# Batch 0 of a linear-attention + MLP kernel: half of Q moved to the GpSimd queue as bf16, and one attention step of batch 1 placed later

## The chip, the cores and the metric

The kernel runs on one core of a Trainium2 chip. The metric is the device time of one execution in microseconds (us); lower is better. The core has a matrix engine (TensorE, "PE", with its weight loads shown apart as "PEld"), a vector engine (VectorE, "DVE"), a scalar engine (ScalarE, "ACT"), a general engine (GpSimd, "POOL") and a sync engine ("SP"). SP, ACT and POOL issue DMA transfers. Transfers that change fp32 to bf16 on the way are all issued by POOL here.

## What is computed

```python
def attention(q, k, v, g_norm):            # batch 8, heads 8, seq 576, head_dim 64
    kv  = einsum('bhsd,bhse->bhde', k, v)
    out = einsum('bhsd,bhde->bhse', q, kv)
    rms = sqrt(mean(out * out, axis=-1, keepdims=True) + 1e-6)
    return out / rms * g_norm

x = attention(...).transpose(0, 2, 1, 3).reshape(4608, 512)
h = x @ w_in                               # 512 -> 2048
g = where(h > 0, h, exp(min(h, 0)) - 1)    # ELU
y = g @ w_out                              # 2048 -> 512, fp32
```

All inputs and the output are fp32 in DRAM. The matrix products run on bf16 copies.

## The kernel before, in words

The 4608 tokens are cut into nine token tiles of 512: the first 512 tokens of each of the eight batches, and one tile that collects the last 64 tokens of every batch. A token tile goes through attention, then `mm1` (the product with w_in: 64 matmuls of 128x512, in eight pieces of eight), ELU, and `mm2` (the product with w_out, 64 matmuls). The order of instructions on each engine is the order in which the Python code emits them; no scheduler changes it. While PE works on the mm1 and mm2 of one tile, the attention steps of the next are put between the pieces.

**The head** is everything before the first mm1 product of batch 0. Q of batch 0 (512 tokens of 8 heads) is brought as fp32 by two transfers of the sync queue, four heads each (`q_raw0`, tile `st_q`, L555). `cast_first` makes bf16 of it on DVE and ACT, one pair of heads at a time, into `q_two`. `turn_first` transposes a pair on PE with four 128x128 transposes (L622), and DVE copies the result from PSUM into `qT0`: pairs 0 and 2 by one copy (L631), pairs 1 and 3 later by `turn_last` (L695). K and V of batch 0 come through POOL, cast to bf16 on the way, as four K chunks and four V chunks of two heads each (`fetch_packed_kv`, L118). Behind them in the same queue stand w_in in seven slices (`load_w_in`, L136), the first part of w_out, Q of batch 1, more of w_out, K and V of batch 1, and so on. POOL has at most eight such transfers under way: the ninth waits until the first has landed, and so forth.

For each of four chunks c of heads PE forms K^T V (`kv_first`, L174, 18 small matmuls), DVE casts it to bf16 (L648), PE multiplies it with `qT0` (`se_first`, L654), ACT squares the scores (`square_first`, L663), PE takes the mean over a head (`mean_first`, L666), ACT takes ln and exp (`log_first` L669, `exp_first` L672), and DVE scales (`scale_first`, L675) and so writes `xT` for the chunk. Chunks 0 and 1 use pairs 0 and 2 of `qT0`, chunks 2 and 3 use pairs 1 and 3. The first 24 mm1 matmuls of batch 0 are emitted by `first` (L684), which starts as soon as chunk 0 of `xT` is there; the other 40 are L467. `idle` (L603) emits matmuls on zeros that nothing reads.

**Batch 1's attention** is interleaved with mm2 of batch 0 (L784 to L820). mm2 is cut by the contraction: `mm2_quarter(0, j, i)` for the first eight slices of w_out, then `mm2(0, j, 8, 10)`, `(10, 12)`, `(12, 14)`, `(14, 16)`, each for the four token groups j. Between these stand `q` (PE transposes of Q, L185), `kvu0`/`kvu1` (K^T V of half the heads each, L174), `seu0`/`seu1` (scores, L373), `sq`, `sum`, `inv`, `mul` (normalising) and `xu0`/`xu1` (PE transposes of the result, L413). POOL's queue brings batch 1's Q, K, V and the slices of w_out in the order in which this stretch uses them.

**The tail** is the last token tile's mm2 (L924): 80 matmuls in five output pieces, each copied out of PSUM by ACT (L932) and stored by two transfers, one from SP and one from ACT (L934). The last two pieces have 256 columns each.

Of the kernel before, what the change touches and what calls it, by code (L numbers as in the profile page):

```python
# [8 lines left out]
FP32 = mybir.dt.float32  # L9
BF16 = mybir.dt.bfloat16  # L10
# [6 lines left out]
def kernel(  # L17
# [13 lines left out]
    nc = tc.nc  # L31
    P = 128

    B, H, S, D = q.shape
    DM = H * D
    DF = moe_w_in.shape[1]
    NPAIR = H // 2
    J = 4
    G = J * P
# [7 lines left out]
    packed = ctx.enter_context(tc.tile_pool(name="packed", bufs=2))  # L47
# [9 lines left out]
    ident = const.tile([P, P], BF16, name="ident")  # L57
# [10 lines left out]
    def stage_tile(tag):  # L68
        return stage.tile([P, 2304], FP32, name=f"st_{tag}", tag=tag)
# [38 lines left out]
    def packed_kv(b):  # L108
        for name, pool in (("k", packed), ("v", qkvp)):
            t = pool.tile([P, 4, RK, D], BF16, name=f"{name}_pk", tag=name)  # L110
            raw[name, b] = t
            bf[name, b] = t.rearrange("p h j d -> p j h d")

    def fetch_packed_kv(name, b, hs=slice(0, 4)):
        in_ = (k if name == "k" else v)[b].rearrange("h r d -> (h r d)").rearrange(
            "(h p x) -> p h x", h=4, p=P
        )
        nc.gpsimd.dma_start(  # L118
            out=raw[name, b].rearrange("p h j d -> p h (j d)")[:, hs], in_=in_[:, hs]
        )  # L120
# [25 lines left out]
    def copy_on(eng, out_, in_):  # L146
        if eng is nc.scalar:
            nc.scalar.copy(out_, in_)
        else:
            eng.tensor_copy(out=out_, in_=in_)  # L150
# [17 lines left out]
    def kv_single(T, kv_ps, u, ls=(0, 1)):  # L168

        for j in range(RK):  # L170
            for l in ls:
                for s in range(2):
                    rows = slice(s * 64, s * 64 + 64)
                    nc.tensor.matmul(  # L174
                        kv_ps[l * 64 : l * 64 + 64, s, u * 64 : u * 64 + 64],
                        lhsT=bf["k", T][rows, j, 2 * u + l, :],
                        rhs=bf["v", T][rows, j, 2 * u + l, :],
                        start=(j == 0),
                        stop=(j == RK - 1),
                    )  # L180
# [328 lines left out]
    def mm2(T, j, f0, f1, hold=False):  # L509

        if f0 == 0 and (T, j) not in o_ps:
            o_ps[T, j] = ps_m2.tile([P, DM], FP32, name="o_ps", tag="mm2")
        for f in range(f0, f1):
            nc.tensor.matmul(  # L514
                o_ps[T, j],
                lhsT=gT[T][:, f, j * P : j * P + P],
                rhs=w_out_sb[:, f, :],
                start=(f == 0),
                stop=(f == FC - 1),
            )  # L520
        if f1 == FC and not hold:
            mm2_out(T, j)

    def mm2_out(T, j):
        if j % 2 == 0:
            o_sb[T] = outp.tile([P, 2, DM], FP32, name="o_sb", tag="o")
        nc.scalar.copy(o_sb[T][:, j % 2, :], o_ps.pop((T, j)))  # L527
        if j % 2 == 1:
            store(T, j // 2)
# [20 lines left out]

    V, A, Q = nc.vector, nc.scalar, nc.gpsimd

    q_raw0 = stage_tile("q")[:, 0:2048].rearrange("p (u x) -> p u x", u=2)
    for u in range(2):
        nc.sync.dma_start(  # L555
            out=q_raw0[:, u].rearrange("p (h x) -> p h x", h=4),
            in_=q[0, 4 * u : 4 * u + 4, 0:G, :].rearrange("h (p j) d -> p h (j d)", j=J),
        )
    packed_kv(0)
    for c in range(4):  # L560
        fetch_packed_kv("k", 0, slice(c, c + 1))
        if c == 2:
            make_identity(nc, ident)
        fetch_packed_kv("v", 0, slice(c, c + 1))
    edges = (0, 256, 512, 768, 1024, 1280, 1664, 2048)
    for lo, hi in zip(edges, edges[1:]):
        load_w_in(slice(lo, hi))
# [14 lines left out]
    for s in range(2):  # L582
# [5 lines left out]
        out=g_row,  # L588
        in_=bass.AP(tensor=g_norm.tensor, offset=g_norm.offset, ap=[[1, 1], [0, 2], [1, 64]]),
# [7 lines left out]
    def bank(n):  # L597
        return ps_head.tile([P, G], FP32, name=f"bank{n}", tag=f"bank{n}")

    def idle(ps, n, dtype=BF16):  # L600
        z = zeros.bitcast(dtype)
        for _ in range(n):
            nc.tensor.matmul(ps, lhsT=z[:, 0:P], rhs=z[:, 0:512], start=True, stop=True)  # L603
# [5 lines left out]
    idle_ps = bank(1)  # L609
    idle(idle_ps, 2, FP32)  # L610
    idle(idle_ps, 1)
    q_st = q_raw0.rearrange("p u (l s j d) -> p u s j l d", l=2, s=2, j=J)
    q_two = attp.tile([P, NPAIR, J, 2, D], BF16, name="q_two", tag="q_two", bufs=1)
    qT0 = attp.tile([P, NPAIR, G], BF16, name="qT", tag="qT")

    def cast_first(pair, eng):
        copy_on(eng, q_two[:, pair], q_st[:, pair % 2, pair // 2])

    def turn_first(ps, pairs):
        for r, pair in enumerate(pairs):  # L620
            for j in range(J):
                nc.tensor.transpose(ps[:, r, j * P : j * P + P], q_two[:, pair, j], ident)  # L622

    def turned(n):
        return bank(n).bitcast(BF16).rearrange("p (r t) -> p r t", r=2)

    cast_first(0, V)
    cast_first(2, A)
    qt_ps = turned(3)
    turn_first(qt_ps, (0, 2))  # L630
    nc.vector.tensor_copy(  # L631
        out=qT0.rearrange("p (s u) t -> p u s t", u=2)[:, 0], in_=qt_ps
    )
    idle(idle_ps, 1, FP32)
    cast_first(1, V)
    cast_first(3, A)

    kv0 = attp.tile([P, 2, 2, D], BF16, name="kv0", tag="kv0", bufs=1)
    x0 = attp.tile([P, KC, G], BF16, name="xT", tag="xT")
# [4 lines left out]
    def kv_first(c):  # L644
        u, l = c // 2, c % 2
        kv_single(0, kv_ps, u, (l,))
        ls = slice(l * 64, l * 64 + 64)
        nc.vector.tensor_copy(out=kv0[ls, u], in_=kv_ps[ls, :, u * 64 : u * 64 + 64])  # L648
# [13 lines left out]
    def square_first(c):  # L662
        nc.scalar.activation(sq0[c], se0[c], AF.Square)  # L663

    def mean_first(c):
        nc.tensor.matmul(mean0[c], lhsT=means, rhs=sq0[c], start=True, stop=True)  # L666

    def log_first(c):
        nc.scalar.activation(r0[c], mean0[c], AF.Ln, bias=eps_col)  # L669
# [4 lines left out]
    def scale_first(c):  # L674
        nc.vector.scalar_tensor_tensor(  # L675
            out=x0[:, c, :], in0=se0[c], scalar=g_col, in1=r0[c], op0=ALU.mult, op1=ALU.mult
        )
# [11 lines left out]
                    stop=(c == KC - 1),  # L689
                )  # L690

    def turn_last(n, pair):
        qt_ps = turned(n)
        turn_first(qt_ps, (pair,))
        nc.vector.tensor_copy(out=qT0[:, pair, :], in_=qt_ps[:, 0, :])  # L695

    g_ps = bank(2)
    nc.tensor.matmul(
        g_ps[:, 0:1],
# [3 lines left out]
        stop=True,  # L703
    )
    nc.vector.tensor_copy(out=g_col, in_=g_ps[:, 0:1])
    kv_first(0)
    turn_last(7, 1)
    se0[0] = bank(6)
    se_first(0)
    square_first(0)  # L710
    turn_last(0, 3)
    kv_first(1)
    mean0[0] = bank(2)
    mean_first(0)
    log_first(0)
# [5 lines left out]
    mean0[1] = bank(0)  # L721
    mean_first(1)
    log_first(1)
    idle_ps = bank(3)
    se0[2] = bank(1)
    se_first(2)
    square_first(2)
    exp_first(1)
    scale_first(0)
    idle(idle_ps, 1)  # L730
    kv_first(3)
    mean0[2] = bank(2)
    mean_first(2)
# [7 lines left out]
    pair = ps_head.tile([P, 2, G], FP32, name="h_ps", tag="kv")  # L741
# [25 lines left out]
    at, ahead = attention(1), attention(2)  # L767
    for i in range(3, 8):
        mm1(0, i, relu=i in (3, 5, 7), home={5: "m2", 6: "at"}.get(i, "m1"))()
    nc.gpsimd.tensor_copy(  # L770
        out=kv_sb[:, 0].rearrange("p (s u) e -> p u s e", s=2), in_=kv0
# [25 lines left out]
    at["mulu0"]()  # L797
    for j in range(J):
        mm2(0, j, 8, 10)
        if j == 2:  # L800
            at["kvu1"]()
    at["seu1"]()
    at["sq1"]()
    at["sum1"]()
    for j in range(J):
        mm2(0, j, 10, 12)
        if j == 1:
            at["inv1"]()
            at["xu0"](scores[:, 0, :])
# [4 lines left out]
        mm2(0, j, 12, 14)  # L814
    for j in range(J):
        mm2(0, j, 14, FC, hold=j > 1)
        if j == 0:
            at["xu1"](scores[:, 1, :])
    mm2_out(0, 2)
    mm2_out(0, 3)  # L820
# [57 lines left out]
    at, ahead = ahead, attention(3)  # L878
# [22 lines left out]
    for T in range(2, NT):  # L901
        at = ahead if T + 1 < NT else None
# [17 lines left out]
    for j, cols in pieces:  # L920
        n = cols.stop - cols.start
        ps = ps_m2.tile([P, DM], FP32, name="o_ps", tag="mm2")[:, 0:n]
        for f in range(FC):
            nc.tensor.matmul(  # L924
                ps,
                lhsT=gT[B][:, f, j * P : j * P + P],
                rhs=w_out_sb[:, f, cols],
                start=(f == 0),
                stop=(f == FC - 1),
            )  # L930
        sb = outp.tile([P, DM], FP32, name="o_last", tag="o_last", bufs=5)[:, 0:n]
        nc.scalar.copy(sb, ps)  # L932
        for l, eng in enumerate((nc.sync, nc.scalar)):
            eng.dma_start(out=rows[l, G:S, j, cols], in_=sb[l * 64 : l * 64 + 64, :])  # L934

# [29 lines left out]
```

## Time and profile before

| what | value |
|---|---|
| median of three runs | 284.0 us (283.41 to 284.29) |
| the profiled execution, its own time | 283.72 us |
| its span in the profile | 282.0 us |
| PE busy | 276.0 us, 98% of the span |
| DVE, ACT, POOL busy | 57%, 55%, 20% |
| chain of work that ended last | 94% PE, 2% DMA, 1% ACT |
| POOL's DMA queue (q0) | 17.30 MB written |
| sync and scalar queues (q1, q10) | 17.83 MB and 0.52 MB |

The span runs from the first to the last instruction of the program that the profiler shows; the execution's own time is 1.72 us longer. Bytes are counted where they are written, so a transfer that casts fp32 to bf16 reads twice what is shown. A row "idle before <-X" says how long an engine stood still before an instruction and what ended that.

### The profile page before, as it was taken

The page shows a single profiled execution, that of the slowest core. Times are in us where ns is not written, and L with a number is a line of the kernel's source. Part 1 is how long each engine was busy: PE and PEld are TensorE (multiplying, and loading weights), DVE is VectorE, ACT ScalarE, POOL GpSimd, SP SyncE. Part 2 cuts the span into 40 slices and gives each one's busy share as a digit, 9 for nine tenths or more (in the row PEclk, how much of TensorE's full clock was granted, in tenths as well). Part 3 has the DMA queues.
Part 4 walks back from the last instruction along what each step waited for, and adds up shares of the span by engine and source line. Part 5 has one row for each costly group of instructions (what it writes and reads, how often), then busy time and mean ns, then how long its engine had stood idle before and what let it go on. Part 6 is the DMA issues. An engine that isn't in the chain of part 4 may idle for free.

```text
span 282.0 us, 5163 instructions
## 1 busy us (share of the span) xinstructions
PE 276.0 (98%) x2134; PEld 129.8 (46%) x2134; DVE 159.8 (57%) x232; ACT 153.8 (55%) x221; POOL 56.2 (20%) x98
## 2 busy tenths in 40 slices
PE   7899999999999999999999999999999999999994
PEld 3444544445444444444444444444444444444444
DVE  2559453888388546843693469445854586444400
ACT  2679546666487438533863377337923692333311
POOL 7854422143421341004110421012000000000000
PEclk9999999999999999999999999999999999999999
DMA  7999999697796696359935795455236123010122
GB/s 196 199 200 202 208 201 191 179 170 128 178 177 114 157 157 156 74 149 121 198 78 148 95 211 73 130 114 148 55 94 76 77 38 112 0 77 0 74 76 74
DMA packets 57579, 35.98 MB, mean 128 GB/s; under 512 B 32852, under 2 KB 55124, under 8 KB 57556
## 3 DMA queue, kind: packets, MB, share of 16 engines
q0 software_dynamic: 21808, 17.30, 41.2%
q1 hardware_dynamic: 35348, 17.83, 24.7%
q10 hardware_dynamic: 400, 0.52, 0.6%
q8 instruction: 16, 0.26, 0.4%
q14 instruction: 7, 0.06, 0.1%
HBM read 36.70 MB, written 9.44 MB: 164 GB/s over the span
## 4 chain that ended last, share of the span: by engine, by line
PE 94%; DMA 2%; ACT 1%; DVE 0%; issue 0%; POOL 0%; POOLq 0%
PE h_ps L467 42%; PE o_ps L514 39%; PE o_ps L924 5%; DMA v_pk<-in_v_dram 2%; PE at L174 2%; PE at L467 1%; PE bank L684 1%; PE at L201 1%; PE h_ps L684 1%; PE se_ps L201 1%; ACT r L669 0%; ACT r L672 0%; PE at L185 0%; ACT sq L663 0%; PE se_ps L413 0%
## 5 line engine op out<-in xcount | busy, mean ns | idle before, releaser
L467 PE MATMUL h_ps<-xT,w_in_sb 128*128 128x512 bf16 x536 | 125.7, 379 | 0.0
L514 PE MATMUL o_ps<-w_out_sb,gT 128*128 128x512 bf16 x512 | 120.5, 379 | 0.0
L479 ACT ACTIVATE elu_e<-h_ps 128x1024 bf16<-128x1024 f32 (+1 forms) x71 | 70.0, 995 | 80.1 <-PE h_ps L467 78.5
L467 PEld LDWEIGHTS <-w_in_sb 128*128 128x128 bf16 x552 | 52.5, 98 | 63.3 <-DVE xT L333 1.7
L514 PEld LDWEIGHTS <-gT 128*128 128x128 bf16 x512 | 49.4, 98 | 58.4
L490 DVE TENSOR_SCALAR elu_e<-elu_e 128x1024 bf16<-128x1024 bf16 (+1 forms) x75 | 31.9, 425 | 73.4 <-ACT elu_e L479 73.4
L498 DVE TENSOR_TENSOR gT<-elu_e,h_ps 128x1024 bf16<-128x1024 bf16 (+1 forms) x51 | 60.1, 1179 | 5.3
L527 ACT COPY o_sb<-o_ps 128x512 f32<-128x512 f32 x32 | 18.6, 586 | 15.5 <-PE o_ps L514 15.5
L218 DVE TENSOR_REDUCE ss<-sq 128x16 f32<-128x1024 bf16 x16 | 19.4, 1218 | 11.1 <-ACT sq L213 10.4
L485 ACT ACTIVATE elu_h<-h_ps 128x1024 bf16<-128x1024 f32 (+1 forms) x20 | 19.5, 990 | 0.0
L150 POOL COPY q_bf<-q_pk 128x512 bf16<-128x512 bf16 x24 | 14.4, 629 | 24.3 <-DMA q_pk<-in_q_dram 24.3
L498 DVE TENSOR_TENSOR gT<-elu_e,elu_h 128x1024 bf16<-128x1024 bf16 x20 | 14.2, 709 | 2.5 <-ACT elu_h L485 1.0
L924 PE MATMUL o_ps<-w_out_sb,gT 128*128 128x512 bf16 (+1 forms) x80 | 14.1, 337 | 0.0
L125 POOL COPY gate<-qT 1x1 bf16<-1x1 bf16 x6 | 1.1, 181 | 58.4 <-DMA qT<-q_bf 58.4
L104 POOL DMA_DIRECT2D q_pk<-in_q_dram x14 | 10.6, 758 | 4.5 <-issue 1.5
L229 DVE TENSOR_TENSOR xs<-at,ss 128x512 bf16<-128x512 f32 x16 | 10.2, 682 | 1.2 <-ACT ss L225 1.2
L924 PEld LDWEIGHTS <-gT 128*128 128x128 bf16 x80 | 7.8, 98 | 6.4 <-DVE gT L498 0.4
L213 ACT ACTIVATE sq<-at 128x1024 bf16<-128x1024 f32 x9 | 9.4, 1043 | 1.6 <-PE at L201 1.0
L118 POOL DMA_DIRECT2D k_pk<-in_k_dram x12 | 8.3, 690 | 3.9 <-DMA w_in_sb<-in_moe_w_in_dram 2.4
L118 POOL DMA_DIRECT2D v_pk<-in_v_dram x12 | 8.2, 683 | 3.2 <-DMA w_out_sb<-in_moe_w_out_dram 1.8
L932 ACT COPY o_last<-o_ps 128x512 f32<-128x512 f32 (+1 forms) x5 | 2.5, 500 | 10.8 <-PE o_ps L924 10.8
L174 PEld LDWEIGHTS <-k_pk 64*64 64x64 bf16 x576 | 6.4, 107 | 4.3 <-issue 4.0
(79 smaller groups left out, 140.7 us busy)
## 6 DMA issues: line engine op xcount, KB each, us to landing
out_dram<-o_sb SPq DMA_DIRECT2D x16, 512.0 KB, 3.3
q_pk<-in_q_dram POOLq DMA_DIRECT2D x14, 256.0 KB, 5.7
k_pk<-in_k_dram POOLq DMA_DIRECT2D x6, 576.0 KB, 8.3
v_pk<-in_v_dram POOLq DMA_DIRECT2D x6, 576.0 KB, 11.6
w_in_sb<-in_moe_w_in_dram POOLq DMA_DIRECT2D x5, 256.0 KB, 7.4
st_q<-in_q_dram SPq DMA_DIRECT2D x2, 512.0 KB, 4.7
w_out_sb<-in_moe_w_out_dram POOLq DMA_DIRECT2D x2, 512.0 KB, 13.9
w_out_sb<-in_moe_w_out_dram POOLq DMA_DIRECT2D x4, 256.0 KB, 12.0
```

What stands on the lines that cost most here:

```text
L118: nc.gpsimd.dma_start(out=raw[name, b].rearrange("p h j d -> p h (j d)")[:, hs], in_=in_[:, hs])
L150: eng.tensor_copy(out=out_, in_=in_)
L174: nc.tensor.matmul(kv_ps[l * 64 : l * 64 + 64, s, u * 64 : u * 64 + 64], lhsT=bf["k", T][rows, j, 2 * u + l, :], rhs=bf["v", T][rows, j, 2 ...
L218: nc.vector.reduce_sum(out=ss, in_=sq.rearrange("p c (h e) -> p (c h) e", h=H), axis=AX.X)
L467: nc.tensor.matmul(h_ps[a][:, cs], lhsT=w_in_sb[:, c, f * P : f * P + P], rhs=x(c, cs), start=(c == 0), stop=(c == KC - 1),)
L479: nc.scalar.activation(e[:, lo:hi, :], ps, AF.Exp)
L485: nc.scalar.activation(h[:, lo:hi, :], ps, AF.Relu)
L490: nc.vector.tensor_scalar(out=e[:, lo:hi, :], in0=e[:, lo:hi, :], scalar1=1.0, scalar2=1.0, op0=ALU.min, op1=ALU.subtract,)
L498: nc.vector.tensor_tensor(out=gT[T][:, 2 * i + lo : 2 * i + hi, :], in0=e[:, lo:hi, :], in1=h, op=ALU.add if relu else ALU.max,)
L514: nc.tensor.matmul(o_ps[T, j], lhsT=gT[T][:, f, j * P : j * P + P], rhs=w_out_sb[:, f, :], start=(f == 0), stop=(f == FC - 1),)
L527: nc.scalar.copy(o_sb[T][:, j % 2, :], o_ps.pop((T, j)))
L924: nc.tensor.matmul(ps, lhsT=gT[B][:, f, j * P : j * P + P], rhs=w_out_sb[:, f, cols], start=(f == 0), stop=(f == FC - 1),)
```

## The change

Of batch 0's Q only heads 0 to 3 are still brought as fp32 by the sync queue. Heads 4 to 7 are brought by a POOL transfer that casts them to bf16 on the way (`q_late`, a `q_pk` buffer); it is issued after two of the four K, V pairs and after the identity matrix is made. Their casts on DVE and ACT go; their transposes become 16 transposes of 128x64 straight from `q_late`, one after the other behind `kv_first(1)`, and one DVE copy writes both pairs of `qT0`. The product that spreads g_norm (`g_ps`) moves behind `kv_first(0)`, an fp32 `idle` of one matmul is dropped, and a bf16 `idle` is added there; another `idle` moves ahead of `se_first(2)`.

In batch 1's attention `kvu1` is emitted one step later (after j = 3 of mm2 8..10, instead of after j = 2), `seu1`, `sq1`, `sum1` after j = 0 of mm2 10..12 instead of before it, and `xu1` after j = 2 of mm2 14..16 instead of after j = 0.

In the tail the last piece is copied out of PSUM half by ACT and half by DVE.

```diff
-    q_raw0 = stage_tile("q")[:, 0:2048].rearrange("p (u x) -> p u x", u=2)
-    for u in range(2):
-        nc.sync.dma_start(
-            out=q_raw0[:, u].rearrange("p (h x) -> p h x", h=4),
-            in_=q[0, 4 * u : 4 * u + 4, 0:G, :].rearrange("h (p j) d -> p h (j d)", j=J),
+    q_raw0 = stage_tile("q")[:, 0:1024]
+    q_late = packed.tile([P, H, J, D], BF16, name="q_pk", tag="q")[:, 0:4]
+
+    def fetch_heads(eng, out_, lo):
+        eng.dma_start(
+            out=out_.rearrange("p (h x) -> p h x", h=4),
+            in_=q[0, lo : lo + 4, 0:G, :].rearrange("h (p j) d -> p h (j d)", j=J),
         )
+
+    fetch_heads(nc.sync, q_raw0, 0)
     packed_kv(0)
     for c in range(4):
         fetch_packed_kv("k", 0, slice(c, c + 1))
-        if c == 2:
+        fetch_packed_kv("v", 0, slice(c, c + 1))
+        if c == 1:
             make_identity(nc, ident)
-        fetch_packed_kv("v", 0, slice(c, c + 1))
+            fetch_heads(nc.gpsimd, q_late.rearrange("p h j d -> p (h j d)"), 4)
...
-    nc.vector.tensor_copy(
-        out=qT0.rearrange("p (s u) t -> p u s t", u=2)[:, 0], in_=qt_ps
-    )
-    idle(idle_ps, 1, FP32)
-    cast_first(1, V)
-    cast_first(3, A)
+    qT_u = qT0.rearrange("p (s u) t -> p u s t", u=2)
+    nc.vector.tensor_copy(out=qT_u[:, 0], in_=qt_ps)
...
-    def turn_last(n, pair):
-        qt_ps = turned(n)
-        turn_first(qt_ps, (pair,))
-        nc.vector.tensor_copy(out=qT0[:, pair, :], in_=qt_ps[:, 0, :])
-
+    kv_first(0)
     g_ps = bank(2)
...
     nc.vector.tensor_copy(out=g_col, in_=g_ps[:, 0:1])
-    kv_first(0)
-    turn_last(7, 1)
+    idle(idle_ps, 1)
     se0[0] = bank(6)
     se_first(0)
     square_first(0)
-    turn_last(0, 3)
     kv_first(1)
+    qt_ps = turned(3)
+    for s in range(2):
+        for j in range(J):
+            for l in range(2):
+                nc.tensor.transpose(
+                    qt_ps[l * 64 : l * 64 + 64, s, j * P : j * P + P],
+                    q_late[:, 2 * l + s, j, :],
+                    ident,
+                )
+    nc.vector.tensor_copy(out=qT_u[:, 1], in_=qt_ps)
     mean0[0] = bank(2)
     mean_first(0)
     log_first(0)
...
-    idle_ps = bank(3)
+    idle(idle_ps, 1)
     se0[2] = bank(1)
     se_first(2)
     square_first(2)
     exp_first(1)
     scale_first(0)
-    idle(idle_ps, 1)
     kv_first(3)
...
     for j in range(J):
         mm2(0, j, 8, 10)
-        if j == 2:
-            at["kvu1"]()
-    at["seu1"]()
-    at["sq1"]()
-    at["sum1"]()
+    at["kvu1"]()
     for j in range(J):
         mm2(0, j, 10, 12)
+        if j == 0:
+            at["seu1"]()
+            at["sq1"]()
+            at["sum1"]()
...
     for j in range(J):
         mm2(0, j, 14, FC, hold=j > 1)
-        if j == 0:
+        if j == 2:
             at["xu1"](scores[:, 1, :])
...
-        nc.scalar.copy(sb, ps)
+        if cols.stop == DM and n < DM:
+            nc.scalar.copy(sb[:, 0 : n // 2], ps[:, 0 : n // 2])
+            nc.vector.tensor_copy(out=sb[:, n // 2 : n], in_=ps[:, n // 2 : n])
+        else:
+            nc.scalar.copy(sb, ps)
```

More of the change, by code (lines that the diff above doesn't have):

```diff
@@ L611 @@
     idle(idle_ps, 1)
-    q_st = q_raw0.rearrange("p u (l s j d) -> p u s j l d", l=2, s=2, j=J)
+    q_st = q_raw0.rearrange("p (l s j d) -> p s j l d", l=2, s=2, j=J)
     q_two = attp.tile([P, NPAIR, J, 2, D], BF16, name="q_two", tag="q_two", bufs=1)
@@ L616, in cast_first @@
     def cast_first(pair, eng):
-        copy_on(eng, q_two[:, pair], q_st[:, pair % 2, pair // 2])
+        copy_on(eng, q_two[:, pair], q_st[:, pair // 2])
     def turn_first(ps, pairs):
```

## The prediction, made before the changed kernel was run

> **What bounds the kernel now.** I read the page first: the engines and the chain of waits. PE is busy for 276.0 of 282.0 us and carries 94% of the chain, so apart from the first microseconds a change counts only if it adds PE idle time or lets the dense matmuls start earlier.
>
> ```profile
> span 282.0 us, 5163 instructions
> PE 276.0 (98%) x2134; PEld 129.8 (46%) x2134; DVE 159.8 (57%) x232; ACT 153.8 (55%) x221; POOL 56.2 (20%) x98
> PEclk9999999999999999999999999999999999999999
> PE 94%; DMA 2%; ACT 1%; DVE 0%; issue 0%; POOL 0%; POOLq 0%
> ```
>
> Next the chain of waits in order of time, 0 to 30 us (start, us, what). The head waits for V's first chunk until 8.03, then runs K^T V, scores, mean, and from 10.42 a row of ACT steps; behind them PE is dense.
>
> ```profile
> 1.92 6.10 DMA v_pk<-in_v_dram
> 8.07 0.48 PE kv_ps L174 x18
> 10.42 0.69 ACT r L669
> 13.78 0.76 DVE xT L675
> 18.33 1.51 PE bank L684 x7
> 19.84 5.18 PE h_ps L467 x24
> ```
>
> Then the timeline of 11 to 30 us: the first mm1 weights are loaded just as w_in lands. DMA and chain are tied there, so advancing one alone gains nothing.
>
> ```profile
> 13.92 0.33 PEld L684 LDWEIGHTS <-w_in_sb 128*128 128x128 bf16 x3 [0.23 <-DMA w_in_sb<-in_moe_w_in_dram]
> 15.16 0.82 PEld L684 LDWEIGHTS <-w_in_sb 128*128 128x128 bf16 x5 [0.26 <-DMA w_in_sb<-in_moe_w_in_dram]
> ```
>
> Why those landings are where they are: the DMA view by queue, for 2 to 4.6, 4.6 to 5.8 and 6.6 to 7.8 us (packets, MB written, share of 16 engines).
>
> ```profile
> q1 hardware_dynamic: 826, 0.83, 92.8%
> ...
> q0 software_dynamic: 104, 0.12, 61.3%
> q1 hardware_dynamic: 173, 0.18, 51.3%
> ...
> q0 software_dynamic: 230, 0.24, 119.8%
> ```
>
> Until 4.6 POOL's queue (q0) moves nothing, though its first K was issued at 1.25; the engines are full of Q. From 4.6 to 5.8 q0 goes at half speed, then at 0.24 MB per 1.2 us, which stays its rate until past 36 us (the rows of the windows view read about 200 GB/s). So everything in POOL's queue lands in order, one byte after another: adding bytes in front delays all behind.
>
> Last, batch 1's attention, the chain for 28 to 48 us. PE has no gap (17.58 busy of 17.58 from 28.48 to 46.06).
>
> ```profile
> 36.49 2.27 PE o_ps L514 x10
> 38.76 0.41 PE at L174 x36
> 39.16 0.54 PE o_ps L514 x2
> 39.70 0.34 PE at L373 x16
> 40.04 0.97 PE o_ps L514 x4
> ```
>
> The x4 begins mm2 10..12. Its w_out slice, issued at 27.74, took 12.1 us: it lands at 39.8, 0.2 before it is used.
>
> **What the Trainium skill says.** "DMA: Bandwidth & Descriptors", section "Issuing engines are not separate DMA queues": transfers of all engines share 16 DMA engines, so moving Q between queues makes no bandwidth. The trace agrees: fp32 Q goes at 386 GB/s from 3 to 4 us, and 200 GB/s written as bf16 are 400 read. Its section "Queues, rings and completion order" says an engine takes turns between queues; before 4.6 the trace shows no turn. "PSUM — Partial Sum Buffer", section "PSUM bank collisions raise a hardware error": two engines must not touch one bank and quadrant at once, ACT and DVE included. That bears on the split copy in the tail; the trace of before has none. "TensorE: Matmul & The Clock Gate", Part 1, lets an idle window of about 3.4 us halve PE's clock; PEclk of before shows no such slice, and its head has no gap that long.
>
> **The change, part by part.**
>
> *Q on the sync queue halved.* 0.52 MB of fp32 goes. Its landing for pairs 0 and 2 (4.48) stays. PE reaches those transposes at 5.49 after the idle matmuls, so nothing is gained there.
>
> *q_late.* POOL issues it as in L104 (0.75 us). That puts off the issues of K, V chunks 2 and 3 by 0.75; about four transfers are queued then, which hides it, otherwise it would cost up to 0.75. The ninth transfer (now the last V) waits for the first K, and w_in for the first V instead: with 0.7 us per chunk there is always a backlog. In the stream it is 256 KB, worth the 1.3 us between the last V's landing (5.66+6.7 = 12.4) and w_in's (7.45+6.3 = 13.7). Everything behind it slides by 1.3, less what POOL's queue wins at its start. One gain is sure: the second Q half no longer shares the engines between 5.8 and 6.6, worth 0.15. The other is the question of this change: when q0 starts. Latest: 4.6 again. Earliest: 2.6, since after an idle spell (issue at 74.31, its issue ending 75.07, no packet until 75.8) q0 moves 0.7 us after the issue's end, and K's ended at 1.93. I take 3.8, where the views above put the end of 0.52 MB of Q: the trace shows q0 starting as the sync queue runs dry, not during it. Gain 0.8. DMA slide: 1.3 - 0.15 - 0.8 = **+0.35** (bounds below).
>
> *The head's chain.* V 0 lands 0.95 earlier, at 7.1, V 1 (2.98+6.5 = 9.5) at 8.55, q_late 1.3 later at 9.85. `mean_first(0)` now stands in PE's queue behind q_late's transposes; behind those two also wait `se_first(1)` and all of chunks 1 to 3. Cost: 0.05 wake-up, 16 transposes at half of L185's row (x32 take 1.01 in the chain), 0.5, and mean 0.35 as in the chain: ACT's first ln at 10.8 instead of 10.42, **+0.4**. From there ACT's row is what it was (ln, square, exp at about 1.64 us per chunk), and the rest follows it: the DMA slide of 0.35 and this are tied again, as before. I take 0.4 once, not twice. The gone casts (0.62 ACT, 0.41 DVE) cost nothing now: ACT stood idle 1.9 us before its cast. The dropped idle (1.24 us of PE) filled a wait for K. The added and moved ones (0.22 each) lie in waits for DVE's kv cast and for ACT. Without that cover, 0.2 each. The DVE copy of both late pairs (0.69, L631's row) runs beside mean and ln; K^T V 2 waits behind it, with 0.3 us to spare.
>
> *Batch 1.* `kvu1` is 0.43 later, which suits a later V. But with `seu1` moved behind, mm2 10..12 is wanted at 36.49 + 2.70 (x12, as the row of twelve at 32.08 in the same view) + 0.41 = 39.6, while its weights land at 39.8 plus 0.05, both shifted alike by the head. PE stands for **+0.25**; before it ran `seu1` (0.34) in that place. Bounds: 0 if PE comes later than the DMA by that much, 0.4 if earlier. `xu1` later: its input is ready about 45.0 (square, sum, inv, mul of 1.02, 1.22, 0.55, 1.29 after 40.7), wanted 45.7: no cost, and its scaled copy (0.75) is wanted only four matmuls into mm1: none.
>
> *Tail.* Last ACT copy of before: 0.37 for 256 columns (L932; 0.59 for 512), so 0.26 for 128. DVE's 128 columns from PSUM: 0.28 (L648). In the program DVE's half waits for ACT's semaphore, as the rule above asks: 0.26 + 0.03 + 0.28 - 0.37 = **+0.2**, and both stores wait for DVE. If they ran beside each other, -0.1. Nothing follows that hides it.
>
> Sum: 0.4 + 0.25 + 0.2 = +0.85, of which I leave 0.05 for overlap: 283.72 + 0.8 = 284.5 for the profiled execution. The median of the runs is 0.28 above that execution: **284.8**.
>
> **Rivals.**
> - *q0 starts no earlier* (4.6, a start-up delay of POOL's own path). For it: no packet in 3.4 us after the first issue, and half speed afterwards, as in the idle start at 75.7 to 76.9 (0.08 MB). Against: the start falls where Q runs out. Slide 1.3 - 0.15 = 1.2; q_late 10.7, first ln 11.65. 1.2 + 0.25 + 0.2 = +1.65: **285.65**.
> - *The other side: q0 starts at 2.6 and shares with Q.* Its price is the bytes: the engines are full from 2.4 us on, and read the same total, so the stream gets ahead by no more than what the mixed stretch and the slow start lose now, 0.3. q_late lands at 9.2, first ln 10.15: -0.3 + 0.25 + 0.2 = +0.15: **284.15**, no slower that can be told. It decides from a start before 3.2.
> - *All hidden*: that, with the two copies of the tail beside each other and no wait for w_out: -0.3 - 0.1 = -0.4: **283.6**. A real gain would need w_in earlier, and its bytes forbid it.
> - *Clock*: PE stands in the longer waits of the head and falls to half speed for a window: 1.7 more, 286.5. Against: the head's longest new gap is about 1 us.
>
> **How the numbers follow.** A measurement of this kernel can tell about 0.3%, 0.85 us, from no change. Middle start (3.2 to 4.2, +0.3 to +1.2): 0.46, split evenly by the bound. Late start: 0.31, slower. Early start: 0.13 and all hidden: 0.03, both the same. Clock or another new wait: 0.04, slower. A gain whose mechanism I don't see: 0.03. So slower 0.58, same 0.39, faster 0.03. Range 283.9 to 286.0, from the early start to the late one and a little beyond; the middle case alone is 284.3 to 285.2.
>
> **What would show it.** In the DMA view q0's first bytes before 4.6 (late start is wrong) or not. q_late landing near 9.85; its transposes, not V, standing ahead of the first mean; the first ln at about 10.8; w_in about 14.05; a PE gap of 0.2 to 0.3 before mm2 10..12, released by w_out; DVE's 128x128 copy after ACT's. I am wrong if the first ln comes before 10.2, if w_in lands before 13.4, or if PE shows gaps elsewhere than these.

## The result, and the profile after

The changed kernel takes **288.45 us**, the median of four runs (288.24 to 289.28); the kernel before takes 283.93 beside it. The ratio is 1.0166, with a 95% interval of 1.0140 to 1.0192. The change costs 4.5 us, where 0.8 was forecast (284.8 from 284.0) and 286.0 was the upper end of the range. In the table of the experiments below, executions more than 1.5% above the fastest of the same kernel are left out: three of e6_syncq (289.02 to 289.81) and two of e7_noq (288.82 and 288.85); with them the medians would be 287.97 and 284.81.

The page of the changed kernel, the lines that answer to those of before:

```profile
span 287.4 us, 5145 instructions
PE 276.5 (96%) x2111; PEld 131.5 (46%) x2141; DVE 160.9 (56%) x231; ACT 153.3 (53%) x220; POOL 57.5 (20%) x99
PEclk9759999999999999999999999999999999999999
PE 91%; DMA 2%; ACT 2%; issue 1%; DVE 1%; POOL 1%; POOLq 0%
```

PE has 23 matmuls fewer in the record and yet is busy 0.5 us longer. The third line says why: the second and third slices (7.2 us each) read 7 and 5 tenths. The clock granted to PE fell near the start; the kernel before has nines throughout. (A nine can also mean that nothing is on record yet, as in the first slice here; the last section returns to this.)

The chain of waits of the changed kernel, head and batch 1 (start, us, what):

```profile
4.07 7.05 DMA q_pk<-in_q_dram
11.16 1.07 PE bank L712 x16
12.23 0.56 PE bank L667
12.81 0.69 ACT r L670
...
17.57 1.82 PE h_ps L685 x4
...
44.71 0.28 ACT kv_sb L352
44.99 0.13 issue
45.12 0.41 PE at L373 x16
```

The wait for `q_late` (until 11.12) stands where the wait for V stood, as forecast, but the first ln comes at 12.81, not at 10.8. Four matmuls of 512 columns need 1.82 us; at the 0.216 us that each of 24 takes in the chain of the kernel before, four need 0.86. In batch 1 no DMA is in the chain.

The timeline of the same kernel, 4 to 20 us, PE (start, us, engine, line, operation, idle before and releaser):

```profile
8.44 0.47 PE L174 MATMUL kv_ps<-v_pk,k_pk 64*64 64x64 bf16 x18
11.16 1.07 PE L712 MATMUL bank<-ident,q_pk 128*64 128x128 bf16 x16 [2.25 <-DMA q_pk<-in_q_dram]
...
12.71 1.11 PE L174 MATMUL kv_ps<-v_pk,k_pk 64*64 64x64 bf16 x18
```

The same 18 small matmuls take 0.47 us before the wait of 2.25 and 1.11 after it.

The stretches in which the clock was constant, read from the trace's clock record, are multiples of 3.41 us long. The windows view, cut at those edges (stretch, length, PE busy, PEld, DVE, ACT, POOL, granted clock, DMA share, GB/s), for the changed kernel and then for the one before:

```profile
7.58:10.99 3.41, 1.22 (x22) 0.59 (x22) 0.45 (x2) 0.60 (x1) 1.63 (x3) 1.00 1.13 164
10.99:14.40 3.41, 3.02 (x38) 1.98 (x39) 0.97 (x2) 1.59 (x3) 3.00 (x5) 0.50 1.34 198
14.40:17.81 3.41, 2.72 (x25) 1.27 (x25) 1.79 (x3) 2.67 (x6) 2.20 (x3) 0.50 1.45 198
17.81:21.23 3.42, 3.42 (x9) 1.22 (x8) 0.75 (x1) 2.24 (x4) 1.67 (x3) 0.50 1.37 200
```

```profile
6.67:10.08 3.41, 3.19 (x51) 1.85 (x50) 2.21 (x6) 1.22 (x2) 2.50 (x4) 1.00 1.20 201
10.08:13.49 3.41, 2.81 (x44) 1.22 (x43) 1.65 (x5) 3.07 (x6) 3.41 (x5) 1.00 1.36 196
```

In the changed kernel PE works 1.22 of 3.41 us in one window, and the three windows after it run at half clock, 10.2 us in all. Everything is lost here: against before, the first ln is 2.39 us later, the 25th mm1 matmul 5.05 (24.73 against 19.68), and the first matmul of batch 1's mm1 still 5.05 (51.11 against 46.06).

### The profile page after: what moved, and what is told of

Read it like the earlier page. It is cut to its first block, busy times and chain, and to the rows that moved or that the text cites. A ratio compares the mean times of both kernels' runs of the same rounds, so it can differ in the third digit from the quotient of the medians.

```text
span 287.4 us, 5145 instructions
## 1 busy us (share of the span) xinstructions
PE 276.5 (96%) x2111; PEld 131.5 (46%) x2141; DVE 160.9 (56%) x231; ACT 153.3 (53%) x220; POOL 57.5 (20%) x99
## 4 chain that ended last, share of the span: by engine, by line
PE 91%; DMA 2%; ACT 2%; issue 1%; DVE 1%; POOL 1%; POOLq 0%
PE h_ps L467 39%; PE o_ps L514 37%; PE o_ps L928 5%; DMA q_pk<-in_q_dram 2%; PE at L174 2%; PE bank L685 1%; PE at L467 1%; PE h_ps L685 1%; PE bank L667 1%; PE at L201 1%; PE se_ps L201 0%; DVE xs L229 0%; DVE ss L218 0%; PE bank L655 0%; ACT sq L664 0%
## 5 line engine op out<-in xcount | busy, mean ns | idle before, releaser
L514 PE MATMUL o_ps<-w_out_sb,gT 128*128 128x512 bf16 x488 | 117.9, 379 | 1.3 <-issue 0.3
L490 DVE TENSOR_SCALAR elu_e<-elu_e 128x1024 bf16<-128x1024 bf16 (+1 forms) x75 | 33.3, 444 | 72.4 <-ACT elu_e L479 72.4
L150 POOL COPY q_bf<-q_pk 128x512 bf16<-128x512 bf16 x24 | 15.3, 666 | 23.5 <-DMA q_pk<-in_q_dram 23.3
L229 DVE TENSOR_TENSOR xs<-at,ss 128x512 bf16<-128x512 f32 x16 | 10.3, 682 | 1.2 <-ACT ss L225 1.2
L174 PEld LDWEIGHTS <-k_pk 64*64 64x64 bf16 x576 | 7.3, 111 | 4.3 <-issue 4.2
L224 ACT ACTIVATE ss<-ss,eps_col 128x16 f32<-128x16 f32 x16 | 5.1, 316 | 3.9 <-DVE ss L218 3.8
```

Source lines behind the costliest of these rows:

```text
L174: nc.tensor.matmul(kv_ps[l * 64 : l * 64 + 64, s, u * 64 : u * 64 + 64], lhsT=bf["k", T][rows, j, 2 * u + l, :], rhs=bf["v", T][rows, j, 2 ...
L490: nc.vector.tensor_scalar(out=e[:, lo:hi, :], in0=e[:, lo:hi, :], scalar1=1.0, scalar2=1.0, op0=ALU.min, op1=ALU.subtract,)
L514: nc.tensor.matmul(o_ps[T, j], lhsT=gT[T][:, f, j * P : j * P + P], rhs=w_out_sb[:, f, :], start=(f == 0), stop=(f == FC - 1),)
```

## The experiments

In words, the theories were these. *Clock*: PE's long wait for `q_late` halves its clock, and the slow stretch is most of the loss. *Landing*: late data alone, of `q_late` or of w_in, is the loss. *Elsewhere*: batch 1 or the tail. Three groups of four ran one after the other: e1 to e4, e5 to e8, f1 to f4. From the second on the question was what in the change lets the clock fall. The median of before, run beside each group, was 283.93 to 284.02.

| label | median, us (range; runs) | ratio to before, 95% |
|---|---|---|
| e1_warm | 287.44 (286.10 to 288.27; 4) | 1.0113 (1.0083 to 1.0143) |
| e2_tail | 284.01 (283.39 to 284.65; 13) | 1.0003 (0.9994 to 1.0012) |
| e3_mid | 284.10 (283.66 to 284.87; 13) | 1.0008 (1.0000 to 1.0017) |
| e4_head | 288.00 (287.81 to 289.36; 4) | 1.0157 (1.0136 to 1.0178) |
| e5_warm2 | 286.53 (286.05 to 288.14; 5) | 1.0086 (1.0069 to 1.0103) |
| e6_syncq | 286.91 (284.42 to 288.31; 7) | 1.0094 (1.0059 to 1.0130) |
| e7_noq | 284.4 (283.53 to 287.78; 16) | 1.0039 (1.0013 to 1.0066) |
| e8_later | 287.87 (285.94 to 288.80; 4) | 1.0130 (1.0090 to 1.0170) |
| f1_noidle | 286.44 (286.11 to 287.12; 6) | 1.0086 (1.0071 to 1.0102) |
| f2_idle | 285.28 (285.02 to 285.81; 5) | 1.0049 (1.0032 to 1.0067) |
| f3_syncq_idle | 284.80 (284.43 to 285.59; 12) | 1.0030 (1.0020 to 1.0039) |
| f4_behind | 290.44 (one execution) | |

### e2_tail, e3_mid, e4_head: one part of the change at a time

e2_tail is the kernel before with the split copy of the tail alone:

```diff
-        nc.scalar.copy(sb, ps)
+        if cols.stop == DM and n < DM:
+            nc.scalar.copy(sb[:, 0 : n // 2], ps[:, 0 : n // 2])
+            nc.vector.tensor_copy(out=sb[:, n // 2 : n], in_=ps[:, n // 2 : n])
+        else:
+            nc.scalar.copy(sb, ps)
```

> The kernel before with the tail's split copy alone. Prediction on record: +0.2 us (DVE's half waits for ACT's half: 0.26 + 0.03 + 0.28 against 0.37). Rival: the halves overlap, -0.1 us. Either is below 0.1% and shows in the profile's rows rather than in the time: 283.8 to 284.3.

e3_mid is the kernel before with the new places of `kvu1`, `seu1`, `sq1`, `sum1` and `xu1` alone:

```diff
-        if j == 2:
-            at["kvu1"]()
-    at["seu1"]()
...
+    at["kvu1"]()
     for j in range(J):
         mm2(0, j, 10, 12)
+        if j == 0:
+            at["seu1"]()
...
-        if j == 0:
+        if j == 2:
             at["xu1"](scores[:, 1, :])
```

> The kernel before with the reordering in batch 1's attention alone (kvu1 one step later, seu1 behind the first of mm2 10..12, xu1 two steps later). Prediction on record: PE stands for 0.25 us before mm2 10..12 because w_out lands at 39.8 and is wanted at 39.6: 284.1 to 284.3. Rival: nothing waits, 283.9; or a gain of up to 0.3 if the old order hid a wait that the trace does not show.

e4_head is the changed kernel with both of these undone:

```diff
-    at["kvu1"]()
+        if j == 2:
+            at["kvu1"]()
...
-        if cols.stop == DM and n < DM:
...
+        nc.scalar.copy(sb, ps)
```

> The changed kernel without its reordering in batch 1 and without the split copy: the change of the head alone. Theory A (the head makes all of it but some 0.2 to 0.4): 288.0 to 288.3, clock 0.98. Rival (the reordering only pays or costs beside the new head, by 0.5 or more): below 287.7 or above 288.8.

Neither of the two small parts can be told from no change, and the head alone costs 4.1 us. Their mechanisms are in the traces. In e2_tail's timeline, 277 to 282 us, DVE's half waits for ACT's:

```profile
277.83 0.27 ACT L933 COPY o_last<-o_ps 128x128 f32<-128x128 f32 x1 [1.37 <-PE o_ps L924]
278.13 0.29 DVE L934 COPY o_last<-o_ps 128x128 f32<-128x128 f32 x1 [11.40 <-ACT o_last L933]
```

From the start of the last matmul to the end of the last copy it is 0.90 us, 0.68 before. In e3_mid's chain, 26 to 50 us, the wait for w_out appears:

```profile
27.37 12.49 DMA w_out_sb<-in_moe_w_out_dram
39.86 0.04 issue
39.90 0.38 PE o_ps L514
```

mm2 10..12 starts with that slice, which lands at 39.86; PE stands idle for 0.25 us before it. Batch 0's first mm2 to batch 1's first mm1 takes 18.04 us there, 17.75 before: 0.29 dearer.

### e1_warm: ten bf16 idle matmuls ahead of q_late's transposes

```diff
     kv_first(1)
+    idle(idle_ps, 10)
     qt_ps = turned(3)
```

> The changed kernel with ten more idle matmuls on zeros (10 x 0.216 = 2.2 us) between K^T V of chunk 1 and the transposes of q_late, so that PE is busy while it waits for q_late (8.9 to 11.16 in the changed kernel's profile). Theory A (PE stands still for 2.2 us, its clock is halved from 11.0 to 21.2, and that makes most of the loss): the clock stays whole, q_late still lands about 11.1, the first ln comes at about 12.1, the dense matmuls follow within 1.6 us of before; 285.6 to 286.2. Rival B (the late stream alone makes the loss, the clock is a bystander): 288 or more, the first mm1 matmul at 17 us or later as in the changed kernel. Rival C (the idle matmuls themselves hold PE past the landing): clock whole, first ln later than 12.8.

It won 1.0 us (its interval and that of the changed kernel just touch, at 1.014) and did not repair the loss. In e1_warm's chain, 0 to 20 us:

```profile
9.45 3.79 PE bank L608 x9
13.24 0.57 PE bank L713 x16
```

The clock was already at half (9.62 to 13.04 in this execution), so the filler took 3.79 us and ran 2.1 us past `q_late`'s landing at 11.14. It filled that window completely (3.42 busy of 3.42), which stayed the only one at half, so the transposes behind it ran at full clock. The filler stood too late: the fall came at the end of the window before it, in which PE was busy for 2.31 us.

### f1_noidle: the kernel before without its fp32 idle

One line of the change, alone:

```diff
-    idle(idle_ps, 1, FP32)
     cast_first(1, V)
```

> The kernel before with one line taken out: the fp32 idle matmul (1.24 us of PE on zeros) that runs while PE waits for K and V of chunk 0. No transfer and no useful instruction changes. Theory A (the dropped idle lets PE's clock fall by itself): executions spread from 284 up to 288 by where the clock's windows fall, as with the changed order and Q on the sync queue (284.4 to 288.3); granted clock 0.98 to 1.0; median 285 to 288. Rival B (the new order on PE or the late Q is needed for it): 283.9, clock whole in every execution.

This one line costs 2.4 us (286.44 against 284.02). f1_noidle's windows view, in the order of columns given above:

```profile
5.69:9.10 3.41, 1.57 (x33) 1.31 (x30) 1.26 (x4) 0.62 (x1) 1.67 (x3) 1.00 1.17 188
9.10:12.51 3.41, 3.36 (x48) 1.97 (x45) 1.25 (x4) 1.47 (x3) 3.41 (x6) 0.50 1.24 187
```

And its timeline, 4 to 13 us, PE:

```profile
8.42 0.47 PE L174 MATMUL kv_ps<-v_pk,k_pk 64*64 64x64 bf16 x18 [1.31 <-DMA v_pk<-in_v_dram]
...
11.54 1.11 PE L174 MATMUL kv_ps<-v_pk,k_pk 64*64 64x64 bf16 x18
```

No Q was moved here. The idle had stood in a wait for V and nothing read what it wrote; without it, PE works 1.57 of 3.41 us and runs at half clock until 19.34. PE's longest single gap after its first matmul is 1.31 us.

### f2_idle: the changed kernel with the fp32 idle put back

```diff
     nc.vector.tensor_copy(out=qT_u[:, 0], in_=qt_ps)
+    idle(idle_ps, 1, FP32)
```

> The changed kernel with that one fp32 idle matmul put back, nothing else. Theory A: it covers PE's wait for V but not the one for q_late (9.0 to 11.1), so the clock still falls in some executions: 286 to 288.5, between the changed kernel (288.45) and the one with both waits filled (286.53). Rival B (only the wait for q_late matters): 288.2 or more in every execution. Rival C (the fp32 idle is all that was missing): 286.0 to 286.6 in every one.

It takes 285.28 us, 3.2 less than the changed kernel, and the two intervals are far apart (1.0067 and 1.0140 at their near ends). f2_idle's windows view:

```profile
6.95:10.36 3.41, 2.42 (x43) 1.25 (x42) 1.06 (x4) 0.60 (x1) 2.25 (x4) 1.00 1.17 157
10.36:13.77 3.41, 2.68 (x58) 1.81 (x59) 1.66 (x3) 2.41 (x5) 3.17 (x5) 1.00 1.31 197
```

Its chain, 0 to 26 us:

```profile
10.36 0.64 PE bank L713 x16
11.00 0.34 PE bank L668
11.33 0.02 issue
11.36 0.69 ACT r L671
```

PE still waits for `q_late` (0.99 us in the timeline), but the clock stays whole, and transposes and mean take 0.98 us instead of 1.63. In the two profiled executions the 25th mm1 matmul is 4.02 us apart (24.73 and 20.71): `q_late`'s landing is 0.80 of it (11.12 and 10.32); transposes and mean are 0.65; first ln to first mm1 1.09; first to 25th mm1 1.48. The last three, 3.22, go with the clock, and come close to the gap of the medians (3.17). These are one execution of each kernel, and that of the changed kernel is itself 0.83 above its median.

### e5_warm2: both fillers

The fp32 idle of f2_idle and the ten idles of e1_warm together.

```diff
+    idle(idle_ps, 1, FP32)
...
     kv_first(1)
+    idle(idle_ps, 10)
```

> The changed kernel with both waits of PE filled: the fp32 idle matmul of the kernel before put back ahead of K^T V of chunk 0 (1.2 us), and ten bf16 idle matmuls (2.2 us at whole clock) behind K^T V of chunk 1. In the run with the ten alone the profiled execution still lost its clock for one window of 3.4 us, from 9.6 on, since the window before it held PE's wait for V. Theory A (clock): now whole in every execution; first ln at about 12.1, since q_late lands at 11.1 whatever PE does; what is left is the late stream: 285.6 to 286.2. Rival B (the late stream alone costs 4 us): 287.5 or more with a whole clock. Rival C (filler in the way): 286.5 to 287.5.

At 286.53 it is 1.25 slower than f2_idle: a filler of this length outlasts the wait that it should fill. In the profiled execution it ends at 12.04, 1.37 us after `q_late` has landed (10.67). There (288.14) the clock even fell later, 16.75 to 20.16. More filler is not safer.

### e6_syncq and f3_syncq_idle: all of Q on the sync queue again

e6_syncq is the changed kernel with heads 4 to 7 brought as fp32 by SP and cast as before, the new order of instructions kept, and no fp32 idle; f3_syncq_idle is the same with that idle.

```diff
+    for u in range(2):
+        fetch_heads(nc.sync, q_raw0[:, u], 4 * u)
...
-            fetch_heads(nc.gpsimd, q_late.rearrange("p h j d -> p (h j d)"), 4)
...
+    cast_first(1, V)
+    cast_first(3, A)
...
+    turn_first(qt_ps, (1, 3))
```

> The changed kernel with heads 4 to 7 of Q brought as fp32 by the sync queue again and cast on DVE and ACT; the place of their transposes (behind K^T V of chunk 1), the dropped fp32 idle, the batch 1 order and the split copy stay as changed. Theory A (the move to POOL's queue makes the loss, through the stream and the wait): landings as before (w_in at 13.7), no wait for Q, first ln at 10.3 to 10.6, 284.0 to 284.6 if the clock stays whole. Rival B (the new order on PE, or the missing fp32 idle with its wait of 1.5 us for V, makes it): clock below 1, 285.5 or more.

> All of the change's new order, batch 1 and the split copy, with heads 4 to 7 of Q on the sync queue as fp32 as before, and with the fp32 idle matmul put back. Theory A (what is left of the change's order is harmless but for the 0.2 of batch 1 and 0.2 of the tail; all else was the move to POOL's queue and the clock): 284.2 to 284.6, clock whole. Rival (the order itself lets the clock fall, since the late transposes and chunk 1 leave other gaps): 285.5 to 288.

e6_syncq lies between 284.42 and 288.31, execution by execution, although no transfer has moved to another queue: without the idle this head is at the edge. With it the spread is gone: 284.80. In f3_syncq_idle the first ln (10.42) and the start of the last matmul (278.06) are where they are in the kernel before. Its loss of 0.8 lies behind that: 0.22 in the tail's copy, and in the profiled execution 3.85 us from the last copy to the end of the span instead of 3.21. The split copy alone does not do this: e2_tail has 3.20 there, and e3_mid 3.21. But the nine traces with both the split copy and the new order of batch 1 all have more: seven have 3.48 to 3.50, e6_syncq 3.66. In f3_syncq_idle the last two stores land 2.7 and 2.9 us after their issue (1.9 and 2.2 in before), with an 8 KB packet of the instruction queue, q14, beside them. Whether that packet is the cause was not tried.

### e7_noq: no transfer for heads 4 to 7

The changed kernel without the `q_late` transfer; the second set of transposes reads heads 0 to 3.

```diff
-            fetch_heads(nc.gpsimd, q_late.rearrange("p h j d -> p (h j d)"), 4)
...
+    turn_first(qt_ps, (0, 2))
```

> The changed kernel without the q_late transfer: heads 4 to 7 take the Q of heads 0 to 3 (their transposes are made again from the first half's bf16 tiles), so 0.5 MB of Q is never read. It asks why POOL's stream came 1.6 us late at w_in instead of 0.35. Theory D (q_late itself is slow: it landed 2.7 us behind V 1 where its bytes are worth 1.3): K 2 lands 0.7 behind V 1, w_in at about 12.6, 2.7 us earlier than in the changed kernel. Rival E (POOL's stream, alone on the engines at its start, is slow whatever stands in it): w_in at about 14.0, only the bytes of q_late (1.3) earlier. Time under D 283.0 to 283.6, under E 283.7 to 284.5, if the clock stays whole.

w_in's first slice lands at 12.84. The order of instructions without `q_late` is therefore ahead of the kernel before in DMA (13.72 there), but its median is 0.5 us higher, and with a whole clock it barely gains. Seven executions lie between 283.53 and 283.73 at a granted clock of 0.997 or more; two others at 0.991 take 285.11, and four at 0.981 to 0.982 take 286.95 to 287.78. The rest lies between. One program on one chip spreads by 4 us along its clock. A mean of 0.982 over 286 us is 0.018 x 2 x 286 = 10.3 us at half clock, three windows of 3.41.

### e8_later and f4_behind: q_late used later, and then also issued later

e8_later moves `q_late`'s transposes behind the scores, means and ln of chunks 0 and 1. f4_behind also issues `q_late` behind all four K, V pairs.

```diff
     kv_first(1)
+    mean0[0] = bank(2)
+    mean_first(0)
+    log_first(0)
...
     qt_ps = turned(3)
```

```diff
         if c == 1:
             make_identity(nc, ident)
-            fetch_heads(nc.gpsimd, q_late.rearrange("p h j d -> p (h j d)"), 4)
+    fetch_heads(nc.gpsimd, q_late.rearrange("p h j d -> p (h j d)"), 4)
```

> The changed kernel with q_late's transposes put behind the scores, mean and ln of chunks 0 and 1, which don't need them (they stood ahead of the first mean). Theory A (what PE does while q_late is under way decides): ACT's first ln at about 9.4 instead of 12.8, PE's wait for q_late shrinks from 2.2 us to under 1, the clock loses fewer windows or none; w_in still lands at 15.4, so the first mm1 matmul starts at about 15.5: 285.5 to 286.3. Rival (the clock falls nonetheless, since PE has little to do in the window): 287 to 288.5.

> The kernel with q_late's transposes behind the scores of chunks 0 and 1, and q_late issued behind all four K, V pairs instead of two. It asks what q_late costs in POOL's stream where the stream has run for longer: behind V 1 it took 1.4 to 2.7 us where the same bytes take 1.3 later on. Theory D (it is slow because it comes while the DMA engines are still out of step after the start): behind V 3 it takes 1.3 to 1.5, and w_in lands at 14.2 to 14.6. Rival E (its shape is slow wherever it stands in the head): 2 or more again, w_in at 15 or later. Its time is worse for the PE, which waits longer for Q: 286 to 289.

In e8_later the first ln stands at 9.54, 0.9 earlier than in the kernel before, and the time is still 287.87: the mean clocks of its executions, 0.994 and 0.982, are worth one and three windows at half clock. In the profiled execution PE does not wait for `q_late` at all: it lands at 10.28 and its transposes begin at 11.23, right behind the second mean. The waits there are for DVE (0.32 us) and ACT (0.93), and still the clock falls. So it does not take a wait for `q_late`. The earlier start of the ACT row did not pay for this. f4_behind has its clock at half as well (one execution, 290.44), and answers another question. Its chain, 0 to 20 us:

```profile
6.17 6.67 DMA q_pk<-in_q_dram
12.83 0.04 issue
12.88 1.06 PE bank L724 x16
```

V3 lands at 11.50 and `q_late` at 12.83: behind all pairs the 256 KB take 1.33 us, the forecast price, and w_in's first slice lands at 14.17, which is e7_noq's 12.84 plus 1.33. Behind two pairs they take more, and not the same each time: 2.72 in the changed kernel, 2.36, 2.06, 1.99, 1.86 and 1.41 in e1_warm, f2_idle, e8_later, e4_head and e5_warm2.

## Why the prediction was wrong

What the 4.5 us are made of, from medians: clock 3.2 (changed kernel less f2_idle), Q by POOL's queue 0.5 (f2_idle less f3_syncq_idle), everything else 0.8 (f3_syncq_idle less before). The sum is 4.4; the other 0.1 is that before was 283.93 in the first group and 284.02 in the last. The 0.5 is likely too small for Q: in the traces the last matmul of f2_idle starts 0.93 us after that of f3_syncq_idle (278.99 against 278.06), and f3_syncq_idle loses 0.35 more behind its last copy.

**The step that failed** is "The dropped idle (1.24 us of PE) filled a wait for K", costed at nothing beside the casts that had the wait as cover. It is true that the wait was there (the idle runs from 6.34 to 7.58, K lands at 7.16 and V at 8.03). But this idle was not cover or load: it was what kept PE's window busy. The view by windows shows how much hung on it: in before, about 0.9 of the 3.19 us that PE is busy in the first window on record are this idle (6.67 to 7.58), and without them some 2.3 are left, before any new wait is counted. f1_noidle prices the step at 2.4 us alone, f2_idle at 3.2 within the change. The prediction asked only what waits for the instruction, and nothing did.

**The clock rival was named and argued away by the wrong quantity.** It was given 1.7 us and a share of a 4% case, because "the head's longest new gap is about 1 us". "TensorE: Matmul & The Clock Gate", Part 1, of the Trainium skill speaks of an idle window of about 3.4 us, and I compared that with gaps. The window length agrees (3.41 in every trace here), but no trace had a gap that long when the clock fell: 2.25 us in the changed kernel, 1.31 in f1_noidle. What went with the fall was the busy share of a window: it fell after 1.22 and 1.57 busy, after 2.31 in e5_warm2 and 2.26 in f4_behind; it held after 2.42 (f2_idle) and 2.81 (before). One row each from the windows views of e1_warm, e4_head and e8_later, where the clock fell next, and of e3_mid and e7_noq, where it held:

```profile
6.21:9.62 3.41, 2.31 (x46) 1.61 (x45) 1.42 (x4) 0.60 (x1) 2.76 (x5) 1.00 1.22 169
5.75:9.17 3.42, 2.39 (x49) 1.65 (x46) 1.16 (x4) 0.59 (x1) 2.97 (x6) 1.00 1.21 172
7.44:10.85 3.41, 2.16 (x28) 1.14 (x27) 0.74 (x3) 1.90 (x4) 2.12 (x4) 1.00 1.21 177
...
10.67:14.08 3.41, 2.48 (x45) 1.41 (x44) 1.57 (x4) 3.41 (x7) 2.88 (x5) 1.00 1.39 196
10.35:13.76 3.41, 2.15 (x39) 1.22 (x33) 1.76 (x5) 3.41 (x7) 2.92 (x5) 1.00 1.42 195
```

e7_noq's 2.15 looks like an exception, but a matmul is missing from its record: the weights of an `idle` are loaded at 11.14, no matmul of it is shown, and PE reads as idle for 0.27 us where it belongs. With these 0.27 the window has 2.42. So in these traces the limit lies near 2.4 of 3.41 us, seven tenths. It is no sharper than that, since records can be missing elsewhere too. The size was wrong too. One window was assumed and three were run, since two half-clock windows with 3.02 and 2.72 busy did not end it.

**q_late's 1.3 us** was right as a price of bytes (f4_behind 1.33) and too small for its place (1.4 to 2.7). That is most of the head's miss at whole clock: in f2_idle `q_late` lands at 10.32 instead of 9.85, and the first ln comes at 11.36, +0.94, where +0.4 stood. The transposes are the rest: 0.64 for 0.5. In the windows view the DMA engines move only 118 and 142 GB/s at 7 to 9 us in the changed kernel, 201 and 203 before. Why the stream is thinner there was not tried and is open.

**When POOL's queue starts**: 3.8 was taken between 2.6 and 4.6. The changed kernel's DMA view for 3.5 to 4.6 us:

```profile
q0 software_dynamic: 143, 0.15, 101.3%
q1 hardware_dynamic: 116, 0.10, 26.4%
```

Nothing of it moves before 3.5, and then it starts as the sync queue runs dry. This step was right, and decided nothing.

**The DMA slide** was +0.35 at w_in (14.05) and is +1.64 (15.36), by `q_late`'s size. It did not matter: the first mm1 weight load in the changed kernel's timeline, 14 to 21 us, names no DMA.

```profile
17.49 0.13 PEld L685 LDWEIGHTS <-w_in_sb 128*128 128x128 bf16 x2 [0.44 <-issue]
```

The chain had moved further than the DMA, so "these two are tied again" was wrong as well. The same holds at whole clock: in f2_idle the slice lands at 14.54 and that load, at 14.96, names no DMA.

**Batch 1**, +0.25: the mechanism and its size were right in e3_mid (0.29), where the slice lands at 39.86. It is a matter of tenths: in f3_syncq_idle, whose head is not later either, the slice lands at 39.38 and the step costs 0. In the changed kernel the slice lands at 40.64, 3.9 us before PE comes to mm2 10..12 (44.58), and the step costs 0, the lower bound given. **The tail**, +0.2: 0.22 in every trace with the split copy. The later end behind that copy was not forecast.

Without the clock the terms stand, in f2_idle's trace, at +0.94 for the head, 0 for batch 1, +0.22 for the tail's copy and +0.29 for the end behind it (3.50 for 3.21), 1.45 together; its median is 1.26 above that of before. No version here beat the kernel before: even e7_noq, which never brings half of Q, has a higher median, and its best execution (283.53) is only 0.4 us below the median of before.

## What to carry to other kernels

An instruction whose result nobody reads is not free to drop: ask what its busy time does, and add up PE's busy time over stretches of 3.4 us before and after the edit, not the longest gap. The windows do not start with the program: the first at full clock begins between 5.37 and 7.58 us in thirteen of the fourteen traces here. If a head is near the limit, its time differs from execution to execution (e6_syncq by 3.9 us), so one profile says little, and the durations of equal matmuls (0.47 or 1.11 us for the same 18) tell the clock better than a mean.

## What was not expected of the hardware

- The clock fell without any PE gap near 3.4 us (1.31 us in f1_noidle), and work alone did not raise it at once: at half clock, windows with 3.02 and 2.72 busy (changed kernel) and 3.36 and 2.72 (f1_noidle) were followed by another at half, each window with 3.42 by full clock, and in e8_later one with 2.82 and in e5_warm2 one with 3.19 too. So what the hardware counts is not just the busy time that the profile shows; what it is stays open.
- The clock record of a trace begins late. In every trace here its first entry is a stretch at full clock, and ahead of it the views read full clock too. The kernel before has its first entry at 6.67 us, f1_noidle at 5.69, and the same eight transposes in their timelines (4 to 14 us of before, then 4 to 13 us of f1_noidle) differ:

```profile
5.49 1.06 PE L622 MATMUL bank<-ident,q_two 128*128 128x128 bf16 x8
...
5.49 0.72 PE L622 MATMUL bank<-ident,q_two 128*128 128x128 bf16 x8
```

In e2_tail, where the record begins at 5.37, they take 0.61. So the nines ahead of the first entry are not a full clock: the kernel before runs slow up to about 6.67 as well, which the prediction's reading of PEclk did not see. In e6_syncq's profiled execution the first entry comes only at 14.49, so that its mean granted clock reads 0.999 although 18 small matmuls at 9.82 had already taken 1.10 us. Two executions of f1_noidle at a mean of 0.999 are nearly as slow (286.1) as those at 0.982 (286.4 to 287.1).
- The same 256 KB cast transfer took 1.41 to 2.72 us behind the landing of its predecessor in one place of the queue, and 1.33 in a later place (f4_behind, one execution).
